# A Fourier-mixing and feed-forward kernel: a new order of work in its opening

## The chip, the cores and the metric

The kernel runs on one core of a Trainium2 chip. A core has a matrix engine (TensorE, PE in the profile, with its weight loads as PEld), three engines for element-wise work (VectorE or DVE, ScalarE or ACT, GpSimd or POOL), and SyncE (SP), which here only issues transfers. Each engine works through its own instructions in order and waits on semaphores that others raise. Transfers are issued by SP and by POOL and are carried out by 16 DMA engines. The metric is the device time of one execution in microseconds; lower is better.

## The reference

```python
# attention block: x is (8, 3008, 256), float32
X = np.fft.fft(x, axis=1)
X = np.fft.fft(X, axis=2)
attn_out = X.real.astype(np.float32)
# feed-forward block on (24064, 256); w_in is (256, 2048), w_out (2048, 256), both float64
h = x @ w_in
relu6 = np.clip(h + 3.0, 0.0, 6.0)
g = h * relu6 / 6.0
return (g @ w_out).astype(np.float32)
```

So: the real part of a two-dimensional Fourier transform over sequence and model dimension, and then a two-layer network with a hard-swish between the layers. The weights arrive as 64-bit floating point numbers, which the kernel turns into 32-bit ones itself.

## The kernel before, in words

**Pairs and stages.** The 8 sequences are worked as 4 pairs (`Pair`, `NP`). A position in a sequence of 3008 is split as 47 × 64. For each pair, `load_x` brings x in eight chunks (`NXC`), each as two transfers on POOL's queue: `load_forward` (a plain one) and `load_partners` (an indirect one, which fetches the mirrored positions by a list of rows, IX). Since only the real part is wanted, a position and its mirror image are added first: `fold` (L160) does that with five additions and subtractions a chunk (four more small ones in the last chunk, number 7). `stage1` (L214) multiplies by the 47-point transform F on PE, `evict_z` (L230) copies the result z to SBUF on ACT and writes it to DRAM (zd), `turn_column` sends one column of it apart (zq). `load_g` (L261) reads it back, with the 64 other positions now on partitions, in six groups of four frequencies; `stage2` (L271) does the 64-point transform with the table T, and `spread` (L290) puts one odd column on all partitions (qn).

**Chunks of the network.** A pair has 12 chunks of 256 columns (`Chunk`), and a chunk has 8 steps (fc). In a step, `mlp1` (L324) multiplies by W1 on PE and gives u and v in PSUM (a ring of three banks, tag uv); Vector forms s (with qn and the column table WN), u + s and v − s; ACT applies a relu to each (L376); Vector's `gate` (L379) makes the activations a of 256 frequencies and of their 256 mirror images. `mlp2` (L395) accumulates the second product over the 8 steps. It uses a scheme of seven products in place of the eight of a 2 × 2 block product: w_out is held in G as seven combinations of its blocks, and `combine` (L381, on POOL) forms four combinations c of the activations. Each product is one matmul of 256 columns. After the eighth step ACT copies the sums to e, `finish` (POOL) puts them together, `store` turns and writes them. The 384 steps of the four pairs run in one list: step s issues `mlp1` of step s + 2, `combine` of s + 1 and `mlp2` of s, and `beside` (L700) places the next pair's x, folds (on POOL), stage 1 and stage 2 between them.

**The weights.** Both weight matrices come in 16 pieces of 128 × 512 numbers (`PIECES`, 0.52 MB each): eight of w_in and eight of w_out. A piece is loaded on POOL's queue (`load_w`), and then converted by four engines in turn: `exponent_a` (ACT, two operations), `exponent_b` (PE, two 16-bit matmuls), `exponent_c` (ACT), `mantissa` (Vector, two operations), and `join` (Vector, multiplies the two). Two pieces of w_in are then multiplied with the transform over the model dimension (`fold_w_in`, four matmuls, wps), copied to W1 by ACT, and one row of the result goes to WN by way of DRAM (two transfers). Two pieces of w_out are combined by `mix_w_out` (L556, four operations on Vector).

**The opening.** For the first pair there is no earlier work to hide anything. The loop over the eight chunks issues `load_x` of chunk c + 2 and `load_w` of piece c + 2, then folds chunk c, converts piece c and does stage 1 of chunk c, so x and weights come in turns. For seven of the eight chunks `fold_first` does only three operations on Vector, and `stage1_first` does the rest of the fold on PE, with four matmuls for each half of a chunk and a negated table FN. Pieces 8 to 14 follow in a second loop, and piece 15 beside the first two steps. `keep_awake` issues matmuls whose result nobody uses. Only when the pieces are through do stage 2 of group 0 and the first `mlp1` run. In this opening the PSUM banks of the later sums (ps_a, four) serve as `bank`.

**What sets the order.** It is written out by hand: each engine runs its instructions in the order in which the code calls them. POOL's queue also holds the x and weight loads; the trace shows a load waiting there until the one eight issues before it has landed.

Of the kernel before, what the change touches and what calls it, by code (L numbers as in the profile page):

```python
# [48 lines left out]
WS = 2.0 ** 20  # L49
N1, N2 = 47, 64  # L50
NK1 = (N1 + 1) // 2

PROD = ("P1", "P2", "-P4", "P5", "P7", "-P6", "P3")
# [3 lines left out]
def kernel(  # L57
# [69 lines left out]
    def x_tile(pr, i):  # L127
        pool, tag = xpool, "x"
        if pr.p == 0 and 4 <= i < 13:
            pool, tag = ((apool, "a"), (cpool, "c"), (spool, "t"))[(i >= 8) + (i >= 11)]  # L130
        return pool.tile([PR + 2, XC, D], F32, tag=tag, name="xt")
# [8 lines left out]
    def load_forward(pr, c):  # L140
        xt = x_tile(pr, 2 * c)
# [9 lines left out]
    def load_partners(pr, c):  # L151
        xr = x_tile(pr, 2 * c + 1)
# [31 lines left out]
    def fold_first(pr, c):  # L184
        xt, xr = pr.x[c][0:PR], pr.xr[c][0:PR]
        r = xr[:, ::-1, :]
        y = ypool.tile([PR, XC + 1, D], F32, tag="y", name="y")
        tt = nc.vector.tensor_tensor
        tt(y[:, 0:XC, 1:P], xt[:, :, D - 1:P:-1], r[:, :, 1:P], op=AL.add)
        tt(xt[:, :, 1:P], xt[:, :, 1:P], r[:, :, D - 1:P:-1], op=AL.add)  # L190
        tt(xt[:, :, 0:P + 1:P], xt[:, :, 0:P + 1:P], r[:, :, 0:P + 1:P], op=AL.add)
        pr.y[c] = y

    def stage1_first(pr, c, i):
        sl = slice(2 * i, 2 * i + 2)
        a, b = pr.x[c][0:PR, sl, :], pr.y[c][:, sl, 1:P]
        ps = bank([P, 2, D], "ps1")
        for k, (f, m, c0) in enumerate([(F[0:PR, 0:PZ], a[:, :, 0:P + 1], 0), (F[0:PR, 0:PZ], b, 1),
                                        (F[0:PR, 0:PZ], a[:, :, 1:P], P + 1), (FN[0:PR], b, P + 1)]):
            nc.tensor.matmul(ps[0:PZ, :, c0:c0 + m.shape[2]], f, m, start=(k == 0), stop=(k > 0),  # L200
                             skip_group_check=True)
        evict_z(pr, c, i, ps)
        if i == XC // 2 - 1:
            del pr.x[c], pr.xr[c]


# [23 lines left out]
    def evict_z(pr, c, i, ps):  # L230
        if i == 0:

            pool, tag = (gpool, "g") if pr.p == 0 and c % 3 == 2 else (zpool, "z")
            pr.z[c] = pool.tile([PZ, XC, D], F32, tag=tag, name="z")
            if c == 0:
                pr.zd = dpool.tile([2, NK1, 2, NS, D], F32, tag="zd", name="zd")
                pr.zq = dpool.tile([2, NK1, 2, NS], F32, tag="zq", name="zq")
# [67 lines left out]
    class Chunk:  # L305
# [3 lines left out]
        def __init__(self, pr, ck):  # L309
            self.pr, self.ck = pr, ck  # L310
            self.last = ck == NCK - 1
            self.final = self.last and pr.p == NP - 1
# [81 lines left out]

    def mlp2(ch, fc):  # L395
# [78 lines left out]
    FN = wpool.tile([PR + 2, PZ], F32, tag="FN", name="FN")  # L474
# [10 lines left out]
    def load_w(j):  # L485
        kind, n, i = PIECES[j]
        st = wpool.tile([P, 2 * WB], I32, tag="st", bufs=4, name="st")
# [23 lines left out]
    def exponent_b(j):  # L511
        ex = ps_h.tile([P, WB], F32, tag="uv", name="ex")
# [17 lines left out]
    def join(j):  # L530
# [8 lines left out]
        b12 = wpool.tile([P, 2, P], F32, tag="b12", bufs=2, name="b12")[:] if i == 0 else None  # L539
        for h, g in enumerate((block(n, 0), b12) if i == 0 else (block(n, 1), block(n, 6))):  # L540
            f, e = (t.rearrange("p (c q h e) -> h p c q e", c=2, h=2, e=DH)[h] for t in (frac, ex))
            nc.vector.tensor_tensor(g.rearrange("p c (q e) -> p c q e", e=DH), f, e, op=AL.mult)
        if i == 0:
            w[PIECES[j]] = b12
# [4 lines left out]
    def use_pair(j):  # L549
        kind, n, _ = PIECES[2 * j]  # L550
        if kind == "in":
            fold_w_in(n)
        else:
            mix_w_out(n)

    def mix_w_out(j):  # L556

        b12 = w.pop(("out", j, 0))
        g = [block(j, i) for i in range(7)]
        tt = nc.vector.tensor_tensor  # L560
        tt(g[3], g[0], b12, op=AL.subtract)
        tt(g[5], g[6], g[3], op=AL.add)
        tt(g[2], g[5], g[1], op=AL.subtract)
        tt(g[4], g[6], b12, op=AL.subtract)

    def fold_w_in(n):
# [4 lines left out]
        for blk in range(2):  # L571
            ps = bank([P, WB], "wps")
# [4 lines left out]
        def copy():  # L577
            for blk in range(2):
                nc.scalar.copy(W1[:, blk, cs], sums[blk][:])
            nc.sync.dma_start(out=wn[n:n + 1], in_=W1[P - 1:P, 1, cs])  # L580

        copies.append(copy)


    def load_wn(n):
        nb = WB // P
        nc.sync.dma_start(out=WN[:, n * nb:(n + 1) * nb], in_=wn[n].rearrange("(j p) -> p j", p=P))
# [6 lines left out]
    def keep_awake(n):  # L594
        ps = ps_h.tile([P, 2 * TB], F32, tag="uv", name="awake")
# [6 lines left out]
    keep_awake(6)  # L602
# [8 lines left out]
    nc.scalar.mul(FN[:], F[:, 0:PZ], -1.0)  # L611
# [10 lines left out]
    wn = dpool.tile([NWI, WB], F32, tag="wn", bufs=1, name="wn")  # L622


    load_forward(first, 0)
    load_partners(first, 0)
    load_w(0)
    load_x(first, 1)
    load_w(1)

    pending, copies = [], []

    def on_scalar(j):
        for i in pending:
            exponent_c(i)
        if j is not None:
            exponent_a(j)
# [3 lines left out]
    def on_vector(j):  # L643
        if j is not None:
            mantissa(j)
        for i in pending:
            join(i)

    def on_tensor(j):
        if j is not None:  # L650
            exponent_b(j)
        done = pending.pop() if pending else 0
        if done % 2:
            use_pair(done // 2)
        if j is not None:
            pending.append(j)

    for c in range(NXC):
        if c + 2 < NXC:
            load_x(first, c + 2)  # L660
        load_w(c + 2)
        if c < NXC - 1:
            fold_first(first, c)
        else:
# [186 lines left out]
```

## Time and profile before

| quantity | value |
|---|---|
| median of 4 runs (lowest to highest) | 1982.1 us (1979.73 to 1984.23) |
| profiled execution, its own time | 1980.91 us |
| its span, first to last instruction | 1979.1 us |
| mean granted PE clock | 0.995 of full speed |
| one fold operation on Vector, 508 elements (L172) | 0.68 us |
| exponent operations on ACT: L509, L518 | 0.75 (two a piece), 0.58 us |
| a wps matmul of 512 columns, two instructions of 0.43 | 0.86 us |
| fetch of x, one transfer of 384 KB, issue to landing, in the steady part (median) | 4.0 us |

The profile's rows have these forms. In the list of waits: engine, line, what it waited for, then the total in us, how many times, and the longest. In the stretches: from and to, length, busy time of PE, PEld, DVE, ACT and POOL with instruction counts, the granted clock, the busy share of the DMA engines and GB/s. In the chain in order of time: start, length, and what the chain ran through. In the timeline: start, length, engine, line and operation, and in brackets the idle time before it and what ended it. A matmul on 32-bit numbers counts as two instructions; their times overlap, so 0.86 us for 512 columns is the distance from one to the next. In the transfers by queue: packets, MB, and the time the packets took as a share of 16 engines over the stretch.

### The profile page before, as it was taken

Reading aid. Unit: us, or ns where it says so; the run is one execution under the profiler, and the core shown is the slowest. Engines: PE = TensorE matmul, PEld = TensorE weight load, DVE = VectorE, ACT = ScalarE, POOL = GpSimd, SP = SyncE. Lnnn points to the kernel's source line nnn. Section 1 sums busy time; section 2 is a strip of 40 time slices with the busy share of each in tenths; the row PEclk is TensorE's granted clock in tenths of the full one; section 3 lists DMA queues with packets and bytes.
Section 4 is the critical chain, followed back from the end, with each engine's and each line's share of the span. In section 5 each row is a group of like instructions: output and inputs, shape, how many; then the busy total and the mean of one; then the engine's idle time right before and its main releaser. Section 6 shows DMA issues by size and latency. Waiting matters only on the chain.

```text
span 1979.1 us, 27746 instructions
## 1 busy us (share of the span) xinstructions
PE 1949.1 (98%) x9178; PEld 1686.8 (85%) x9178; DVE 1435.1 (73%) x2775; ACT 688.0 (35%) x1164; POOL 1412.5 (71%) x1604
## 2 busy tenths in 40 slices
PE   9899999999999999999999999999999999999998
PEld 5488888888998888888898888888889888888887
DVE  5677767776787776776777776777678777777776
ACT  6533333333333333333333333333333333333332
POOL 4277778786687787777768877778667667666765
PEclk9999999999999999999999999999999999999999
DMA  9502211121112111120111221212110101111000
GB/s 283 160 25 62 51 40 46 48 50 35 27 36 51 41 48 49 51 62 24 36 33 30 63 50 47 57 41 54 37 22 22 30 13 26 26 24 28 17 20 20
DMA packets 149701, 93.31 MB, mean 47 GB/s; under 512 B 121739, under 2 KB 135055, under 8 KB 149558
## 3 DMA queue, kind: packets, MB, share of 16 engines
q1 hardware_dynamic: 139294, 57.86, 12.3%
q0 software_dynamic: 9472, 33.49, 6.1%
q8 instruction: 72, 1.18, 0.3%
q14 instruction: 71, 0.58, 0.1%
q10 hardware_dynamic: 792, 0.20, 0.0%
HBM read 54.19 MB, written 37.33 MB: 46 GB/s over the span
## 4 chain that ended last, share of the span: by engine, by line
PE 93%; DVE 2%; ACT 1%; issue 0%; DMA 0%; SPq 0%; DVEq 0%; ACTq 0%
PE acc L403 56%; PE v L334 16%; PE u L334 16%; PE ps L284 2%; PE ps L227 2%; DVE a L379 1%; DVE s L339 1%; ACT t L376 0%; ACT PM L509 0%; DVE o L461 0%; PE wps L574 0%; DVE u L360 0%; DMA out_dram<-o 0%; PE ps L224 0%; PE awake L597 0%
## 5 line engine op out<-in xcount | busy, mean ns | idle before, releaser
L393 POOL TENSOR_TENSOR c<-a 128x512 f32<-128x512 f32 (+1 forms) x383 | 477.7, 1247 | 434.5 <-PE acc L403 371.7
L403 PE MATMUL acc<-c,G 128*128 128x256 f32 (+1 forms) x3072 | 712.1, 375 | 0.0
L376 ACT ACTIVATE t<-u,half 128x512 f32<-128x512 f32 (+1 forms) x384 | 260.7, 679 | 1101.8 <-DVE u L349 1022.0
L403 PEld LDWEIGHTS acc<-c,G 128*128 128x128 f32 x3072 | 577.9, 190 | 72.7
L339 DVE SCALAR_TENSOR_TENSOR s<-qn,WN,u 128x256 f32<-128x256 f32 (+1 forms) x768 | 330.4, 472 | 355.3 <-PE u L334 355.0
L403 PE MATMUL acc<-a,G 128*128 128x256 f32 (+1 forms) x2304 | 552.1, 375 | 0.0
L403 PEld LDWEIGHTS acc<-a,G 128*128 128x128 f32 x2304 | 434.3, 190 | 55.9
L334 PE MATMUL v<-q,W 127*128 127x256 f32 (+1 forms) x1536 | 390.0, 376 | 4.5 <-DVE a L379 4.4
L334 PE MATMUL u<-q,W 128*128 128x256 f32 (+1 forms) x1536 | 388.9, 376 | 2.4 <-DVE a L379 2.1
L379 DVE SCALAR_TENSOR_TENSOR a<-t,u 128x512 f32<-128x512 f32 (+2 forms) x448 | 264.1, 601 | 103.9 <-ACT t L376 101.8
L334 PEld LDWEIGHTS u<-q,W 128*128 128x128 f32 x1536 | 286.2, 190 | 58.2 <-issue 14.8
L334 PEld LDWEIGHTS v<-q,W 127*128 127x128 f32 x1536 | 288.6, 190 | 45.1 <-DVE a L379 4.1
L393 POOL TENSOR_TENSOR c<-c,a 128x256 f32<-128x256 f32 (+1 forms) x383 | 274.3, 716 | 30.0
L393 POOL TENSOR_TENSOR c<-a,c 128x256 f32<-128x256 f32 (+1 forms) x383 | 274.1, 716 | 30.0
L349 DVE TENSOR_TENSOR u<-s,v 128x512 f32<-128x512 f32 x352 | 245.0, 696 | 37.7 <-PE v L334 0.8
L379 DVE SCALAR_TENSOR_TENSOR a<-t,v 128x512 f32<-128x512 f32 (+1 forms) x480 | 263.8, 566 | 0.0
L376 ACT ACTIVATE t<-v,half 128x512 f32<-128x512 f32 (+1 forms) x384 | 260.3, 678 | 0.0
L351 DVE TENSOR_TENSOR v<-v,s 128x512 f32<-128x512 f32 x352 | 244.2, 694 | 0.0
L393 POOL TENSOR_TENSOR r<-w,e 128x256 f32<-128x256 f32 (+1 forms) x94 | 90.7, 986 | 3.7
L411 ACT ACTIVATE e<-acc 128x512 f32<-128x512 f32 (+2 forms) x190 | 86.2, 544 | 3.4 <-PE acc L403 3.3
L461 DVE STREAM_TRANSPOSE o<-r 128x256 f32<-128x256 f32 (+1 forms) x192 | 72.5, 416 | 0.2
L239 ACT COPY z<-ps 96x512 f32<-96x512 f32 x64 | 37.1, 580 | 82.6 <-PE ps L227 63.4
(91 smaller groups left out, 779.2 us busy)
## 6 DMA issues: line engine op xcount, KB each, us to landing
out_dram<-o SPq DMA_DIRECT2D x746, 32.0 KB
zd<-z SPq DMA_DIRECT2D x32, 384.0 KB
g<-zd SPq DMA_DIRECT2D x48, 256.0 KB
xt<-in_x_dram POOLq DMA_DIRECT2D x21, 384.0 KB, 4.0
qn<-qd SPq DMA_DIRECT2D x19, 256.0 KB
st<-in_moe_w_in_dram POOLq DMA_DIRECT2D x8, 512.0 KB, 11.1
st<-in_moe_w_out_dram POOLq DMA_DIRECT2D x8, 512.0 KB, 4.9
xt<-in_x_dram POOLq DMA_DIRECT2D x7, 376.0 KB, 4.0
```

The lines of the kernel that those rows point to most:

```text
L227: nc.tensor.matmul(ps[0:PZ], F[0:PR, 0:PZ], y[:, 2 * i:2 * i + 2, :], start=True, stop=True)
L284: nc.tensor.matmul(ps[:, blk, u * P:n].rearrange("p (b k) -> p b k", b=2), g[:, kk, blk * (P + 1):blk * (P + 1) + P], T[:, :, gr, blk, kk, ...
L334: nc.tensor.matmul(ps[:, i, 0:nq], W1[r, blk, f * P:(f + 1) * P], q[r, blk, of:of + nq], start=True, stop=True)
L339: nc.vector.scalar_tensor_tensor(s[:, i, 0:nq], qn[:, of:of + nq], WN[:, f:f + 1], u[:, i, 0:nq], op0=AL.mult, op1=AL.add)
L349: nc.vector.tensor_tensor(u[:], s[:], v[:], op=AL.add)
L351: nc.vector.tensor_tensor(v[:], v[:], s[:], op=AL.subtract)
L376: nc.scalar.activation(t, h, AF.Relu, bias=half[:], scale=scale)
L379: nc.vector.scalar_tensor_tensor(dst, t, 1.0, h, op0=AL.min, op1=AL.mult)
L393: (eng or nc.gpsimd).tensor_tensor(out, in0, in1, op=AL.add)
L403: nc.tensor.matmul(ch.acc[i // 2][:, i % 2, 0:ch.n], G[:, i, fc, :], mv, start=(fc == 0 and i % 2 == 0), stop=(fc == NF - 1), skip_group_c ...
L411: nc.scalar.mul(ch.e[:, k:i + 1, 0:ch.n], ch.acc[i // 2][:, 0:i + 1 - k, 0:ch.n], 1.0 / WS)
L461: nc.vector.transpose(o[:, 0:n // DH, h], ch.r[:, m, h, 0:n].rearrange("p (j i) -> p j i", i=DH))
```

## The change

Only the opening and the first chunk of the first pair change; the order of the steps after that is as before, with the next pair's loads placed a little differently beside the first pair.

- x comes first: six chunks of x and half of the seventh are issued before any weight, starting with chunk 7; the rest and weight pieces 0 to 3 follow after the first two folds, pieces 4 to 6 after the folds of chunks 3 and 4 (they use other buffers).
- `fold_first` and `stage1_first` go: every chunk is folded on Vector alone by `fold`, and stage 1 is the plain matmul. One `keep_awake` matmul follows each chunk.
- After x, pieces 0 to 4 are converted one after the other (with two `keep_awake` matmuls each), then come stage 2 of group 0, `spread`, and the first `mlp1`. Pieces 5 and 6 stand before the first step, three pieces (7 to 9, 10 to 12) in each of the first two steps, two in the third, one in the fourth (`DUE`).
- The first chunk uses eight plain block products (`mlp2_first`: four matmuls of 512 columns a step), which need no `combine`, no `finish`, and of G only the four plain blocks. It issues `mlp1` one step ahead. `mix_w_out` moves from Vector to POOL, into steps 4 to 6 and 9.
- WN is filled by four direct transfers for each `fold_w_in` instead of two through DRAM.

```diff
-    def fold_first(pr, c):
...
-    def stage1_first(pr, c, i):
...
+    def mlp2_first(ch, fc):
+        a = ch.a.pop(fc)
+        for h in range(2):
+            if fc == 0:
+                ch.acc[h] = ps_a.tile([P, 2, TB], F32, tag="acc", name="acc")
+            for f in range(2):
+                nc.tensor.matmul(ch.acc[h][:], G[:, (B11, B12, B21, B22)[2 * f + h], fc, :], a[:, :, f],
+                                 start=(fc == 0 and f == 0), stop=(fc == NF - 1 and f == 1))
+        if fc == NF - 1:
+            ch.r = epool.tile([P, 2, 2, TB], F32, tag="r", name="r")
+            for h in range(2):
+                for m in range(2):
+                    nc.scalar.mul(ch.r[:, m, h], ch.acc[h][:, m], (1 - 2 * m) / WS)
...
+        pool, tag, bufs = (wpool, "st", 4) if j % 7 < 4 else (cpool, "c", None)
+        st = pool.tile([P, 2 * WB], I32, tag=tag, bufs=bufs, name="st")
...
-        tt = nc.vector.tensor_tensor
-        tt(g[3], g[0], b12, op=AL.subtract)
+        tt = nc.gpsimd.tensor_tensor
+        tt(g[4], g[B22], g[B12], op=AL.subtract)
...
-            nc.sync.dma_start(out=wn[n:n + 1], in_=W1[P - 1:P, 1, cs])
+            nb = WB // P
+            for k in range(nb):
+                f = n * nb + k
+                nc.sync.dma_start(out=WN[:, f:f + 1], in_=W1[P - 1:P, 1, f * P:(f + 1) * P])
...
-    keep_awake(6)
+    keep_awake(9)
...
+    def head(j):
+        exponent_a(j)
+        mantissa(j)
+
+    def tail(j):
+        exponent_b(j)
+        exponent_c(j)
+        join(j)
+        if j + 7 < len(PIECES):
+            load_w(j + 7)
+        if j % 2 and PIECES[j][0] == "in":
+            folds.append(PIECES[j][1])
...
+    order = [NXC - 1] + list(range(NXC - 1))
+    for c in order[0:6]:
+        load_x(first, c)
+    load_forward(first, order[6])
+    for k, c in enumerate(order):
+        for part in range(2):
+            fold(first, c, part, nc.vector)
+        for i in range(XC // 2):
+            stage1(first, c, i)
+        keep_awake(1)
+        if k == 0:
+            load_partners(first, order[6])
+        elif k == 1:
+            load_x(first, order[7])
+            load_t(0)
+            for j in range(4):
+                load_w(j)
+        elif k in (4, 5):
+            for j in ((4, 5), (6,))[k - 4]:
+                load_w(j)
     load_g(first, 0)
+    head(0)
+    for j in range(5):
+        exponent_b(j)
+        keep_awake(2)
+        exponent_c(j)
+        fold_all()
+        if j < 4:
+            head(j + 1)
+        join(j)
+        copy_all()
+        load_w(j + 7)
+        if j % 2 and PIECES[j][0] == "in":
+            folds.append(PIECES[j][1])
     for i in range(2):
         stage2(first, 0, i)
     spread(first, 0)
...
+    DUE = [(7, 8, 9), (10, 11, 12), (13, 14), (15,), (), (), (), ()]
+    head(5)
     mlp1(*chunk(0))
-    mlp1(*chunk(1))
+    tail(5)
+    head(6)
+    keep_awake(3, spare[0])
+    tail(6)
...
+        if s < NF:
+            for j in DUE[s][:1]:
+                head(j)
+            copy_all()
+            mlp1(*chunk(s + 1))
+            for j in DUE[s][:1]:
+                tail(j)
+            for j in DUE[s][1:2]:
+                head(j)
+            mlp2_first(*chunk(s))
+            for j in DUE[s][1:2]:
+                tail(j)
+            for j in DUE[s][2:]:
+                head(j)
+            fold_all()
+            for j in DUE[s][2:]:
+                tail(j)
+            if 4 <= s < NF - 1:
+                mix_w_out(s - 4)
+            if s == NF - 1:
+                mlp1(*chunk(NF + 1))
+                combine(*chunk(NF))
```

## The prediction

> **What bounds the kernel now.** I read the page first: engines' busy time, then the chain of work that ended last.
>
> ```profile
> span 1979.1 us, 27746 instructions
> ...
> PE 1949.1 (98%) x9178; PEld 1686.8 (85%) x9178; DVE 1435.1 (73%) x2775; ACT 688.0 (35%) x1164; POOL 1412.5 (71%) x1604
> ...
> PE 93%; DVE 2%; ACT 1%; issue 0%; DMA 0%; SPq 0%; DVEq 0%; ACTq 0%
> ```
>
> From about 110 us on, PE (TensorE) never waits: the end is the moment at which steady steps begin, plus a fixed amount of matmul work. The change touches the opening, so I read the busy time in stretches of 10 us, whose last three columns are the granted PE clock, the DMA share and GB/s.
>
> ```profile
> 10.00:20.00 10.00, 8.79 (x25) 5.80 (x26) 5.96 (x12) 4.74 (x8) 4.94 (x8) 0.66 1.03 264
> 20.00:30.00 10.00, 10.00 (x40) 6.20 (x39) 5.75 (x12) 7.03 (x14) 3.90 (x6) 1.00 1.04 280
> 50.00:60.00 10.00, 8.03 (x27) 4.16 (x28) 7.59 (x18) 7.12 (x14) 2.14 (x3) 1.00 0.94 298
> 80.00:90.00 10.00, 5.73 (x21) 3.83 (x20) 7.62 (x14) 4.81 (x8) 4.17 (x5) 0.88 0.12 26
> 90.00:100.00 10.00, 10.00 (x37) 8.32 (x37) 5.86 (x11) 2.24 (x4) 5.45 (x6) 0.78 0.25 73
> ```
>
> The transfer engines are full until about 60 us. Then, in order of time, the chain (start, us, what):
>
> ```profile
> 61.65 1.42 ACT PM L509 x2
> ...
> 63.48 3.43 PE wps L574 x8
> ...
> 77.01 1.78 PE ps L284 x16
> 78.79 0.91 PE ps L295 x8
> ...
> 88.35 2.07 PE u L334 x4
> 90.42 1.71 PE v L334 x4
> 92.13 4.25 PE acc L403 x14
> ...
> 98.11 3.02 PE acc L403 x14
> ...
> 130.15 3.02 PE acc L403 x14
> ```
>
> Three numbers follow. The first mlp1 starts at 78.79 + 0.91 = 79.7. The eighth step's products end at 133.2, so the first chunk takes 53.5 us: eight steps of 4.74 (0.86 + 0.86 + 3.02) are 38; the rest is waits at 82 to 92 and 106 to 110, and the half clock around 88 to 94. All later work is equal in both kernels except where I name it.
>
> **The change, part by part.** A: until x has been folded. The waits name the limit, and the timeline dates it:
>
> ```profile
> DVE y L189 <- DMA xt<-in_x_dram,IX: 14.2, 7, 6.1
> ```
> ```profile
> 9.79 0.68 DVE L189 TENSOR_TENSOR y<-xt 94x508 f32<-94x508 f32 x1 [6.06 <-DMA xt<-in_x_dram,IX]
> ...
> 42.66 0.68 DVE L189 TENSOR_TENSOR y<-xt 94x508 f32<-94x508 f32 x1 [1.58 <-DMA xt<-in_x_dram,IX]
> ```
> ```profile
> q0 software_dynamic: 320, 1.16, 74.0%
> ```
>
> Folds begin at 9.8, 14.6, 19.5 and 24.5: 4.85 us for one chunk of x (0.79 MB) and one weight piece (0.52 MB). Without the piece, by bytes, a chunk is 2.9 us. But the last row (the POOL queue from 48 to 52 us, no x in it) moves 1.16 MB in 0.74 × 4 us, 392 GB/s: there a piece costs 1.34 us, which leaves 3.5 for the chunk. I take 3.3, nearer the second, because its row has weights alone. z writes (0.39 MB, 1.0 to 1.2 us each) share the engines from the third chunk on; five or six fall before the last x, and T's first group costs 1.1 more. The last chunk lands at 9.9 + 7 × 3.3 + 5.5 × 1.0 + 1 = 39.5 us (before: 48). Vector now does 5 operations a chunk, four of 0.68 overlapping to 2.65 us, 3.0 in the odd chunk with its four extra ones: under 3.3, so hidden by the transfers except after the last. POOL issues x without the pieces in between; the two x loads that need a folded chunk's buffer are queued after the first two folds (13 and 16 us), while over 3 MB are still in flight, so they cost nothing; if those transfers ran faster they would cost what the issue needs, under 2 us. The four weight loads behind them on POOL, and the next three, hold up nothing that is needed sooner. PE's work on x falls from 1.73 to 0.86 a bank (fold on Vector instead of the FN products), all of it under the transfers before and after; so do the three more awake matmuls at the start and the eight between the chunks.
>
> B: five pieces before the first step. After the last x: fold 2.65, stage 1 on PE 1.72 (two of 0.86), z copy and column on ACT 0.9, so the first exponent (L509) starts at 44.8; 1.41 and 0.4 later its matmuls are done, 46.6. From there a piece without a fold costs the chain's ACT to PE to ACT turn, 2.36 (68.73 to 71.09 in the timeline); with a fold PE holds it: two awake matmuls 1.72, wps 3.43, ex 0.45 = 5.6; the last has no next ex, 5.15. Sum 46.6 + 3 × 2.36 + 5.6 + 5.15 = 64.4, then stage 2 and spread 1.78 + 0.91: the first mlp1 starts at 67.1. Group 0's load is issued when the last z has landed, about 50 (before, 5.4 us after the z write), and 0.5 MB lands near 55: hidden by the folds of the weights. WN's direct 512-byte transfers have no row; an x load that had the engines to itself, 768 times as long, landed 4.0 us after its issue (the median of the page's list of transfers), so each lands at most that long after the copy that ends at 65. The multiply-add that needs it is due at 69: I take nothing, bounds 0 and 1. SP now issues sixteen WN transfers (0.4 to 0.6 each) instead of eight, with group 1's loads and T's behind them; these are needed at step 7, 40 us on. Gain of the opening: 79.7 − 67.1 = 12.6 us.
>
> C: the first chunk. PE per step: mlp1 1.73 and four products of 512 columns at 0.86, 3.44 instead of 3.02, so 5.2 us; no combine on POOL, which removes the 1.27 + 0.73 + 0.73 wait ahead of the c products. But eleven pieces are now converted inside it, each 2.0 on ACT (1.41 + 0.58), 1.8 on Vector (0.43 + 0.69 + 0.69), 0.45 on PE. They stand in line with the step's own: two relu 1.38 on ACT, 3.55 on Vector, and each `exponent_b` is queued on PE ahead of the products, each `exponent_c` on ACT behind the relus. Laid out along ACT: 7.0 from the first mlp1 to piece 6's `exponent_c` (qn copy 0.6, then 3.3 to the end of the first relus, 0.6 + 1.4 + 0.45 + 0.6 for the rest). In a step, a piece takes a turn of 1.41 + 0.45 + 0.58 = 2.45. The step's first `exponent_c` waits behind the relus, which wait for mantissa 1.1, s 0.85, u and v 1.3: 3.45 after its exponent instead of 0.45, so +3.0. Where a weight fold of 3.43 stands on PE ahead of the third ex, it ends 1.45 after that exponent. Steps 0 and 1: 3 × 2.45 + 3.0 + 1.45 = 11.8 each (step 1's W1 copies, 1.16 on ACT, fall into the 3.0); step 2: 2 × 2.45 + 3.0 = 7.9; step 3 is level with PE, 5.3; then PE bounds, three of 5.2 and one of 6.1 with group 1's stage 2. Sum 65.5 us. POOL's `mix_w_out` in steps 4 to 6 and 9 (four of 0.73) meets an idle POOL, and takes 1.7 per pair off Vector; the slow ones of before at 101.6 to 105 (0.83 to 1.48 each beside POOL's work, and 2.3 us of PE wait behind them) go.
>
> Still owed at that point: mlp1 of step 9, 1.73, which before had already run, and group 1's second stage-2 half, 0.89. And three mlp1 now stand almost back to back (steps 8 to 10) on three uv buffers; the third waits for the gates of the first: 1.5 (bounds 0 and 2.1, the wait at 86). So C costs 65.5 + 1.7 + 0.9 + 1.5 − 53.5 = +16.1.
>
> The clock: PE sat idle 2.15 us before 11.2, and the clock fell to 0.66 in that stretch; idle 2.1 us before 88.35 with 1.8 shortly ahead, and it fell to 0.78. Two us before 50.8 cost nothing. The new opening has PE idle about 1.8 us in every 4.4 while x arrives (stage 1 1.72 + awake 0.86 busy). If the last of these chunks runs at half clock it costs 1.7; if the first weight fold does too, 1.7 more. Bounds 0 and 3.4; I take 0.9, a quarter.
>
> The Trainium skill speaks here, "TensorE: Matmul & The Clock Gate", Part 1: PE falls to half clock after at least one idle window of about 3.4 us. By that rule no gap of the new opening is long enough, and the sum would be 0.9 lower; the rows above show the fall after gaps of 2.1 us, so the rows decide.
>
> Sum: −12.6 + 16.1 + 0.9 = +4.4 us on the profiled execution's 1980.9 (span 1979.1 and 1.8 around it), that is 1985.3. Its time is 1.2 under the median 1982.1, so against the median: 1986.5. A measurement can hardly tell 0.2%, 4 us.
>
> **The rivals.** 1, on the other side: x alone runs faster than between weights. If a chunk took the 2.0 us of the 392 GB/s row, the last would land at 9.9 + 7 × 2.0 + 6.5 = 30.4, and its fold would end at 33 instead of 42 (Vector alone, 7 × 2.65 after the first, allows 31.5). The weights follow in time: pieces 0 to 4 at 1.34 us each and two z writes are there by 40. 9 us earlier is 1977.5. It decides from 2.6 us a chunk on (7 × 0.7 = 4.9 us against the 4.4). For it: 392 GB/s is reached; against: four intervals in a row fit 3.3 to 3.5.
> 2, the clock falls in the first chunk too: steps 0 to 2 leave PE gaps of 1.0 to 1.5. The fall at 88 held into the next stretch, and cost u, v and acc (2.07 + 1.71 + 4.25 against 0.86 + 0.86 + 3.02) 3.3 us. Once here and in full while x arrives: 1986.5 − 0.9 + 3.3 + 3.4 = 1992. For it: the gaps are many; against: three awake matmuls are placed there, and a gap of 1.8 alone at 82.8 cost nothing.
> 3, the order doesn't change in effect: z writes delay x so that it lands at 46, as before. Then the opening gains 6 us, 1993. Against it: the writes are 3 MB of 9.5.
>
> **How the numbers follow.** Forecast 0.50, rival 1 0.28, rival 2 0.18, rival 3 0.04. The forecast's own spread is the x price (2.9 to 3.5: −2.8 to +1.4), the clock (−0.9 to +2.5), the uv wait (−1.5 to +0.6) and 2 us for the layout: 1981 to 1991, half of it beyond 1986.1 (the median and 0.2%). So slower 0.27 + 0.22 = 0.49; within 0.2% 0.23 + 0.16 = 0.39; faster, from rival 1 at its full price, 0.12. The range takes in most of rivals 1 and 2: 1978 to 1993.
>
> **What would show it.** Folds (now L170) starting 3.3 apart, then 4.3, the last near 39.5; first L509 at 45; first u matmul at 67; PE gaps of about 1 us before ex in steps 0 and 1, each step 11.8; u of step 10 waiting for a gate. The prediction is wrong if the last fold starts before 35 or after 43, if steps 0 and 1 take under 10 or over 13 us, or if the clock falls between 65 and 105.

## The result and the profile after

The changed kernel takes 1985.27 us (median of 39 runs, 1983.75 to 1988.12), the kernel before 1981.01 us beside it: a ratio of 1.002, 95% interval 1.0016 to 1.0025. It is 4.3 us slower, 0.2%; the prediction had called that hard to tell, and over this many runs it is clear. The forecast was 1986.5, and its sum for the difference was +4.4 us. The profiled execution took 1985.56 us, with a span of 1983.8.

So the difference came out to 0.1 us. The parts did not: several missed, and by luck they cancel. The page of the changed kernel first (busy time, then shares of the chain that ended last):

```profile
span 1983.8 us, 27522 instructions
...
PE 1951.8 (98%) x9076; PEld 1665.7 (84%) x9076; DVE 1437.3 (72%) x2773; ACT 687.4 (35%) x1163; POOL 1398.2 (70%) x1591
...
PE 93%; DVE 3%; DMA 2%; ACT 1%; issue 1%; POOL 0%; SPq 0%; DVEq 0%; ACTq 0%
```

PE is busy 2.7 us longer and the span is 4.7 us longer; DMA has gone from 0 to 2% of the chain. Two lines of the chain in order of time make up more than half of that, 22.45 us (start, us, what):

```profile
18.42 10.45 DMA zd<-z
...
30.04 12.00 DMA zd<-z
```

Those are writes of z. The prediction had expected the landing of x to set the opening, and the folds of x in Vector's timeline show that x is early:

```profile
9.89 0.55 DVE L170 TENSOR_TENSOR xt<-xt 94x381 f32<-94x381 f32 x1 [6.07 <-DMA xt<-in_x_dram,IX]
...
22.56 0.68 DVE L170 TENSOR_TENSOR xt<-xt 94x508 f32<-94x508 f32 x1 [0.39 <-DMA xt<-in_x_dram,IX]
...
33.79 0.68 DVE L170 TENSOR_TENSOR xt<-xt 94x508 f32<-94x508 f32 x1 [1.36 <-DMA xt<-in_x_dram,IX]
```

The last fold starts at 33.8, not 39.5. ACT's timeline shows who waits instead:

```profile
28.95 1.06 ACT L220 COPY z<-ps 96x512 f32<-96x512 f32 x2 [3.75 <-DMA zd<-z]
...
39.28 1.06 ACT L220 COPY z<-ps 96x512 f32<-96x512 f32 x2 [7.32 <-DMA zd<-z]
...
42.12 1.07 ACT L220 COPY z<-ps 96x512 f32<-96x512 f32 x2 [1.44 <-DMA zd<-z]
...
43.43 1.37 ACT L508 ACTIVATE PM<-st,bias 128x512 uint8<-128x512 int16 x2
```

A z copy needs a free z buffer. A buffer is free when its write to DRAM has landed, and these landed 10 to 12 us after their issue. ACT waits 12.5 us in three places, and the first exponent, which stands behind the last z copy on ACT, starts at 43.4. PE meanwhile has nothing to do. Its rows, and the granted clock in the stretches of 10 us (the third number from the end):

```profile
44.21 1.22 PE L513 MATMUL ex<-PM,E 128*128 128x512 f16 x2 [4.73 <-ACT PM L508]
...
67.26 1.03 PE L316 MATMUL u<-q,W 128*128 128x256 f32 x4
...
75.91 3.59 PE L385 MATMUL acc<-a,G 128*128 128x512 f32 x8
...
80.45 0.85 PE L513 MATMUL ex<-PM,E 128*128 128x512 f16 x2 [0.95 <-DVE wi L534]
...
87.39 3.59 PE L385 MATMUL acc<-a,G 128*128 128x512 f32 x8
...
98.85 3.59 PE L385 MATMUL acc<-a,G 128*128 128x512 f32 x8
...
106.52 3.59 PE L385 MATMUL acc<-a,G 128*128 128x512 f32 x8
...
135.80 1.13 PE L316 MATMUL v<-q,W 127*128 127x256 f32 x4 [1.54 <-DVE a L361]
```
```profile
10.00:20.00 10.00, 9.25 (x28) 3.93 (x28) 8.79 (x20) 2.93 (x6) 6.43 (x8) 1.00 1.03 246
20.00:30.00 10.00, 8.47 (x20) 2.86 (x19) 7.68 (x16) 3.98 (x8) 4.34 (x7) 1.00 1.04 313
30.00:40.00 10.00, 7.45 (x17) 2.54 (x16) 7.05 (x14) 2.38 (x7) 1.15 (x2) 1.00 1.03 363
40.00:50.00 10.00, 5.74 (x11) 2.32 (x11) 1.96 (x4) 5.97 (x12) 1.08 (x2) 0.66 0.98 356
...
70.00:80.00 10.00, 8.88 (x26) 4.09 (x24) 9.09 (x18) 7.35 (x12) 1.79 (x3) 1.00 0.54 150
```

The first mlp1 starts at 67.26 (forecast 67.1). Products of steps 0 to 3 start at 75.9, 87.4, 98.9 and 106.5: intervals of 11.48, 11.46 and 7.67 (forecast 11.8, 11.8, 7.9). The clock falls to 0.66 between 40 and 50, behind the idle 4.73 us, and is 1.00 from 50 on.

The last part of the difference lies later, where the prediction had not looked. In both kernels a few matmuls of the next pair's stage 1 wait for ACT. Before, then after, PE's timeline:

```profile
270.03 1.10 PE L227 MATMUL ps<-y,F 94*96 94x512 f32 x2 [0.67 <-ACT q L287]
...
453.25 1.10 PE L227 MATMUL ps<-y,F 94*96 94x512 f32 x2 [0.57 <-ACT q L287]
...
553.31 0.90 PE L334 MATMUL v<-q,W 127*128 127x194 f32 x4 [0.48 <-DVE a L379]
```
```profile
190.81 1.10 PE L208 MATMUL ps<-y,F 94*96 94x512 f32 x2 [0.68 <-ACT q L268]
...
273.00 1.10 PE L208 MATMUL ps<-y,F 94*96 94x512 f32 x2 [0.68 <-ACT q L268]
...
355.20 1.10 PE L208 MATMUL ps<-y,F 94*96 94x512 f32 x2 [0.68 <-ACT q L268]
...
437.39 1.10 PE L208 MATMUL ps<-y,F 94*96 94x512 f32 x2 [0.68 <-ACT q L268]
...
557.73 0.89 PE L316 MATMUL v<-q,W 127*128 127x194 f32 x4 [0.20 <-DVE a L361]
```

Beside the first pair there are four such places instead of two. The last row of each fence is the same matmul of the first pair's last chunk, and so a common mark: 557.73 − 553.31 = +4.4 us. Later batches add 0.2.

### The profile page after: what moved, and what is told of

The parts are those of the page before. It is cut to its first block, busy times and chain, and to the rows that moved or that the text cites. A ratio compares the mean times of both kernels' runs of the same rounds, so it can differ in the third digit from the quotient of the medians.

```text
span 1983.8 us, 27522 instructions
## 1 busy us (share of the span) xinstructions
PE 1951.8 (98%) x9076; PEld 1665.7 (84%) x9076; DVE 1437.3 (72%) x2773; ACT 687.4 (35%) x1163; POOL 1398.2 (70%) x1591
## 4 chain that ended last, share of the span: by engine, by line
PE 93%; DVE 3%; DMA 2%; ACT 1%; issue 1%; POOL 0%; SPq 0%; DVEq 0%; ACTq 0%
PE acc L401 55%; PE v L316 16%; PE u L316 16%; PE ps L265 2%; PE ps L208 2%; DMA zd<-z 1%; PE acc L385 1%; DVE a L361 1%; DVE s L321 1%; ACT t L358 0%; ACT PM L508 0%; DMA xt<-in_x_dram,IX 0%; DVE o L459 0%; PE wps L563 0%; PE spare L563 0%
## 5 line engine op out<-in xcount | busy, mean ns | idle before, releaser
L375 POOL TENSOR_TENSOR c<-a 128x512 f32<-128x512 f32 (+1 forms) x375 | 467.4, 1246 | 409.1 <-PE acc L401 360.6
L401 PE MATMUL acc<-c,G 128*128 128x256 f32 (+1 forms) x3008 | 696.9, 374 | 0.0
L401 PEld LDWEIGHTS acc<-c,G 128*128 128x128 f32 x3008 | 565.4, 190 | 71.1
L401 PE MATMUL acc<-a,G 128*128 128x256 f32 (+1 forms) x2256 | 539.1, 375 | 0.0
L401 PEld LDWEIGHTS acc<-a,G 128*128 128x128 f32 x2256 | 424.2, 190 | 54.4
L375 POOL TENSOR_TENSOR c<-c,a 128x256 f32<-128x256 f32 (+1 forms) x375 | 268.4, 716 | 29.4
L375 POOL TENSOR_TENSOR c<-a,c 128x256 f32<-128x256 f32 (+1 forms) x375 | 268.2, 715 | 29.4
L208 PE MATMUL ps<-y,F 94*96 94x512 f32 x120 | 61.3, 601 | 9.5 <-ACT q L268 5.2
```

What stands on the lines that cost most here:

```text
L208: nc.tensor.matmul(ps[0:PZ], F[0:PR, 0:PZ], y[:, 2 * i:2 * i + 2, :], start=True, stop=True)
L375: (eng or nc.gpsimd).tensor_tensor(out, in0, in1, op=AL.add)
L401: nc.tensor.matmul(ch.acc[i // 2][:, i % 2, 0:ch.n], G[:, i, fc, :], mv, start=(fc == 0 and i % 2 == 0), stop=(fc == NF - 1), skip_group_c ...
```

## The experiments

The theory from the two traces: z's buffers hold the opening, by some 4 us; the half clock behind them costs 1 to 2 us; the eleven conversions inside the first chunk cost more than anything else; and stage 1 stands too close behind stage 2. Rivals are named with each run. Each time carries the ratio to the kernel before with its 95% interval. The kernel before was measured again beside each group of runs, and its median lay between 1981.0 and 1982.7 us; so a difference of under 2 us between two runs is read only where the traces show it.

**1. More z buffers.** Three chunks of the opening put their z into buffers of another pool that is still unused.

```diff
+            if pr.p == 0 and c in (3, 5, 6):
+                pool, tag = qpool, "q"
             pr.z[c] = pool.tile([PZ, XC, D], F32, tag=tag, name="z")
```

> The changed kernel with three of the first pair's eight z tiles in the q buffers, which nothing uses before stage 2, so that no z copy waits for an earlier z to have landed in DRAM. Theory 1, the opening ends late because ACT's z copies wait for the z writes (12.5 us in three waits, the last x is folded at 36.4 but the first exponent starts at 43.4): the waits go, the first exponent starts at 37.5 to 38.5, PE's idle time after the last stage 1 falls from 4.7 us to under 2, the clock stays at 1.00, first u matmul at 59 to 61 instead of 67.4, total 1977 to 1979, 6 to 8 us under the changed kernel and 2 to 4 under the one before. Theory 2, as in the prediction, the arrival of x and the weights sets the opening: the copies start earlier but the exponents wait for weight pieces instead, the first u matmul stays within 2 us of 67.4, total 1983 to 1986.

Measured 1981.02 us (1.0000, 0.9991 to 1.0009), 4.2 us under the changed kernel. The waits for z's writes are gone, and ACT's timeline shows the next one, on the four buffers of the copied column, whose small writes stand in the same queue:

```profile
35.91 0.30 ACT L237 ACTIVATE zc<-z,F 96x4 f32<-96x4 f32 x1 [2.59 <-DMA zq<-zc]
...
38.88 0.30 ACT L237 ACTIVATE zc<-z,F 96x4 f32<-96x4 f32 x1 [1.72 <-DMA zq<-zc]
39.09 1.38 ACT L510 ACTIVATE PM<-st,bias 128x512 uint8<-128x512 int16 x2
```

The first exponent comes 4.3 us sooner, the first mlp1 at 62.80 instead of 67.26. The cause is settled: the opening waited for z buffers. The gain fell short of the expected time (1977 to 1979), because of this second wait and because x's own end is close by: the last fold starts at 31.7, from which copies without any wait would lead to a first exponent at 37.0. The expectation also had PE's idle time under 2 us and the clock at 1.00. The idle time is 2.49 us, and the four awake instructions behind it take 3.43 us instead of 1.88:

```profile
39.88 0.38 PE L515 MATMUL ex<-PM,E 128*128 128x512 f16 x1 [2.49 <-ACT PM L510]
...
40.74 3.43 PE L587 MATMUL awake<-Z,ones 128*128 128x512 f32 x4
```

**2. The clock.** Five awake matmuls in PE's idle time ahead of the first exponent, nothing else.

```diff
     load_g(first, 0)
+    keep_awake(5)
```

> The changed kernel with five more idle matmuls of 0.86 us after the last stage 1, which bridge PE's 4.7 us gap. If the half clock of 44 to 49 us (an ex of 1.22 and two awake matmuls of 3.53 in place of 0.8 and 1.88) lies on the path, the first u matmul comes 1.5 to 2.0 us earlier, at 65.5, and the total falls by as much, to about 1983.5. If the ACT chain hides it, no change.

Measured 1984.42 us (1.0014, 1.0005 to 1.0023), 0.9 less than the changed kernel; the two intervals overlap, so the trace has to show it. The clock is 1.00 from 40 to 50, with the z waits as long as before (13.4 us). ACT's first exponent and PE's first mlp1:

```profile
43.89 1.38 ACT L508 ACTIVATE PM<-st,bias 128x512 uint8<-128x512 int16 x2
```
```profile
66.14 1.03 PE L316 MATMUL u<-q,W 128*128 128x256 f32 x4
```

The first mlp1 starts 1.1 us sooner although the first exponent started 0.5 later: the way between them takes 22.25 us instead of 23.83. The half clock is real and worth 1.6 us there.

**3. No conversions in the first chunk.** Pieces 7 to 15 are neither loaded nor converted (G, W1 and WN are filled with zeros first), so part of the weights is left out of the result; pieces 5 and 6 stay.

```diff
     def head(j):
+        if j >= 7:
+            return
...
     def tail(j):
+        if j >= 7:
+            return
...
```

> The changed kernel without pieces 7 to 15: they are neither loaded nor converted, and the blocks of W1, WN and G that would hold them are zero from memory sets on POOL in the opening. It measures what the eleven conversions cost the first chunk. Theory of the prediction (three conversions in a step make a chain over ACT, PE and Vector of 11.8 us instead of PE's 5.2): the first chunk, from the first u matmul to the end of the eighth step's products, falls from 64.3 us to about 50, steps 0 to 3 take 5.2 each, total 14 us lower, near 1971. Rival (the first chunk is bound by its eight products and by mlp1 one step ahead): under 4 us lower.

Measured 1969.2 us (0.9937, 0.9922 to 0.9952). The first mlp1 starts at 66.88, nearly where it was, the steps take 5.17 us each, and the products of step 7 start at 112.03 instead of 128.07. With 0.38 taken off for the earlier start, nine conversions and the two weight folds that go with them cost the first chunk 15.7 us, 1.7 a piece. That is the price that the change pays for an opening that is 12.3 us shorter.

**4. Two pieces a step.** The nine pieces spread 2, 2, 2, 2, 1 instead of 3, 3, 2, 1.

```diff
-    DUE = [(7, 8, 9), (10, 11, 12), (13, 14), (15,), (), (), (), ()]
+    DUE = [(7, 8), (9, 10), (11, 12), (13, 14), (15,), (), (), ()]
```

> The changed kernel with the eleven pieces of the first chunk spread as 2, 2, 2, 2, 1 over its first steps (after the two around the first mlp1) instead of 3, 3, 2, 1. Theory: the third piece of a step costs 11.47 - 7.67 = 3.8 us because the step's second and third exponents wait in line behind its own relus and the weight fold; two pieces cost 7.7. Then steps 0 to 3 take 7.7 each and step 4 about 5.3: 36 us instead of the 41 that the changed kernel's steps 0 to 4 take, so 1980 to 1981, 4 to 5 us faster. Rival: ACT's and Vector's work for eleven pieces is the limit wherever they stand; then the first chunk keeps its 64 us and the time stays at 1985.

Measured 1988.77 us (1.0033, 1.0020 to 1.0046): slower, a miss. PE's timeline has the products of steps 0 to 4 start at

```profile
75.79 3.60 PE L385 MATMUL acc<-a,G 128*128 128x512 f32 x8
...
86.63 3.60 PE L385 MATMUL acc<-a,G 128*128 128x512 f32 x8
...
99.33 2.84 PE L385 MATMUL acc<-a,G 128*128 128x512 f32 x6 [2.04 <-DVE G L540]
...
104.81 3.59 PE L385 MATMUL acc<-a,G 128*128 128x512 f32 x8
...
112.82 3.60 PE L385 MATMUL acc<-a,G 128*128 128x512 f32 x8
```

(step 2 at 96.26, with the 2.04 us of wait inside it). From step 0 to step 4 that is 37.0 us, against 35.8 in the changed kernel (75.91 to 111.68). A piece of w_out that moves to the head of its step makes the products wait for its join. The theory "a third piece costs 3.8 us because it is the third" falls: spread this way, the same work costs no less. The profiled execution took 1986.47 us, less than the other five, and its trace explains 1.1 us; the rest of the median's 3.5 stays open.

**5. The gap before the first chunk of the kernel before.** Two awake matmuls in each of two places around its first mlp1s, to see whether its idle 2.1 us cost it the half clock.

```diff
     mlp1(*chunk(0))
+    fill(2)
     mlp1(*chunk(1))
     on_tensor(15)
+    fill(2)
```

> The kernel before with two idle matmuls between its first two mlp1 and two after piece 15's exponent matmuls, where PE waits at 82.8 to 84.7 and 86.2 to 88.4. If the half clock at 88 to 94 comes from these gaps and lies on the path, u, v and the first products of that stretch take 0.9, 0.9 and 3.0 us instead of 2.07, 1.71 and 4.25, and the total falls by about 3 us, to 1978. If the clock falls for another reason, no change or up to 1 us more.

Measured 1978.99 us (0.9982, 0.9972 to 0.9993). In the stretches and in PE's timeline of this run:

```profile
80.00:90.00 10.00, 9.34 (x48) 6.79 (x47) 6.23 (x13) 5.26 (x9) 1.77 (x2) 1.00 0.20 62
90.00:100.00 10.00, 9.59 (x43) 7.81 (x42) 7.67 (x14) 3.48 (x6) 7.89 (x10) 1.00 0.26 79
```
```profile
91.14 1.13 PE L334 MATMUL u<-q,W 128*128 128x256 f32 x4 [0.41 <-DVE a L379]
92.11 1.03 PE L334 MATMUL v<-q,W 127*128 127x256 f32 x4
```

The clock stays at 1.00; u and v take 0.97 and 0.87 instead of 2.07 and 1.71, and acc 3.02 instead of 4.25. 3 us of the kernel before were half clock behind its two gaps of 1.84 and 2.12 us. Both were filled here, so the run does not say which of them did it.

**6. Weights issued later.** In program order, all seven pieces of the opening behind the seventh fold.

```diff
-            for j in range(4):
-                load_w(j)
-        elif k in (4, 5):
-            for j in ((4, 5), (6,))[k - 4]:
+        elif k == 6:
+            for j in range(7):
                 load_w(j)
```

> All seven weight pieces of the opening are issued after the seventh chunk's fold instead of after the second to the sixth, so x and the z writes have the transfer engines to themselves. Theory: z writes land 10 to 12 us after their issue because the weights behind x keep the engines full; without them they land 4 to 6 us after it, and ACT's waits for a z buffer (12.5 us together in the changed kernel) fall under 4 us, the last chunk's copies start near 37 instead of 39.3. The first weights then land at about 33 to 36, after the last fold, and the first exponent starts between 37 and 40 instead of 43.4, the kernel 2 to 5 us faster than the changed one (1981 to 1983). Rival: a z write takes its 10 us whatever else is in flight; then the waits stay at 12 us and the kernel stays at 1985 or, with the weights late, becomes slower.

Measured 1985.89 us (1.0015, 1.0006 to 1.0025), ACT's waits unchanged at 12.5 us. It decides nothing, since the edit moved almost nothing: the first piece is issued at 22.42 instead of 21.51, because POOL runs through its list ahead of the folds and is held by earlier landings only.

**7. Weights really held back.** The same, with a small POOL copy that reads the sixth folded chunk ahead of them.

```diff
+        if k == 5:
+            seen = wpool.tile([P, 1], F32, tag="seen", bufs=1, name="seen")
+            nc.gpsimd.tensor_copy(seen[0:PR], first.y[c][:, 0, 0:1])
```

> The changed kernel with the opening's seven weight pieces held back by a small copy on GpSimd that reads the sixth folded chunk: the pieces are then issued from about 29 on, where the changed kernel issues six of them from 21.5 to 30 whatever its program order, since an issue waits for the landing of an earlier transfer. Theory: the z writes are late (10 to 12 us after their issue) because they share the engines with eight loads in flight; with x alone in flight from 21 to 29 and its queue running empty, the third to sixth land 5 to 7 us after their issue, ACT's three waits for a z buffer (12.5 us together) fall below 6, the first exponent starts at 39 to 41 instead of 43.4 unless the first weights, due near 35, are late: 1981 to 1983. Rival: the writes are slow by themselves; the waits stay at 12 us and the time at 1985 or above.

Measured 1981.56 us (0.9996, 0.9987 to 1.0005), 3.7 less than the changed kernel, and the first exponent at 39.80, both as expected. But the waits fall only to 8.4 us, and the chain of waits still shows slow writes:

```profile
19.39 9.99 DMA zd<-z
...
30.55 7.86 DMA zd<-z
```

The first was issued and landed before any weight piece was in flight; POOL's timeline has the first pieces at

```profile
29.62 2.16 POOL L489 DMA_DIRECT2D st<-in_moe_w_in_dram  x4
```

The second, with weights behind x now in flight, took 7.86 us where it had taken 12.00. So weights that come sooner make later writes slower, but beside x alone a write needs 10 us too.

**8. Column buffers as well.** Run 1 with eight column buffers instead of four, and three awake matmuls ahead of the first exponent.

```diff
-        zc = zpool.tile([PZ, XC], F32, tag="zc", bufs=4, name="zc")
+        zc = zpool.tile([PZ, XC], F32, tag="zc", bufs=8, name="zc")
...
+    keep_awake(3)
```

> On top of the run with three more z buffers: eight buffers instead of four for the copied columns, and three awake matmuls ahead of the first exponent. Theory: with z no longer the limit, the columns' four buffers were (waits of 2.6 and 1.7 us on ACT before the last chunks); without them the first exponent starts at about 37 instead of 39.1 and the first mlp1 near 60.5 instead of 62.8, and the three matmuls save another 0.5 to 1 us of half clock: 1978 to 1979. Rival: the next wait behind it is the landing of the last z write and so of group 0; then stage 2 waits and the first mlp1 stays at 62 to 63, the time at 1981.

Measured 1981.15 us (0.9995, 0.9986 to 1.0005): no gain over run 1, a miss. No buffer wait is left, but in this run the last x landed later and the awake matmuls held up the first ex. Rows of Vector and ACT:

```profile
34.09 0.68 DVE L170 TENSOR_TENSOR xt<-xt 94x508 f32<-94x508 f32 x1 [1.67 <-DMA xt<-in_x_dram,IX]
```
```profile
39.77 1.39 ACT L510 ACTIVATE PM<-st,bias 128x512 uint8<-128x512 int16 x2
...
42.82 0.58 ACT L519 ACTIVATE ex<-ex 128x512 int32<-128x512 f32 x1 [1.66 <-PE ex L515]
```

The last fold starts at 34.1, against 31.7 in run 1. Of these 2.4 us, 1.1 are there at the first fold (10.06 against 8.97), before any z was written; that the z writes, which now go out sooner, take the rest from x is likely but was not shown. Now the landing of x is the limit that the prediction had supposed. The rival named for this run, the landing of group 0, was not it.

**9. Stage 1 one step later.** Beside the changed kernel's later steps only.

```diff
-                    put(t + 8 + 3 * i, stage1, nx, c, i)
+                    put(t + 9 + 3 * i, stage1, nx, c, i)
```

> The changed kernel with the next batch's stage 1 one step later in the later chunks, so that it no longer stands in the same step right behind a stage 2 of the present batch. Theory: of the 4.3 us that the changed kernel is slower, 1.4 are two more waits of 0.68 us of PE for the copy of stage 2's bank (at 190.8 and 355.2, beside the one at 273 that the kernel before has at 270); all three go, 2.0 us faster: 1983. Rival: the waits were slack of PE that is given back later (a buffer that comes free in time); then the time stays at 1985.

Measured 1980.7 us (0.9988, 0.9979 to 0.9998), 4.6 less than the changed kernel; 2.0 had been expected. Of the eight places in all, six are gone: PE's timeline has none of the four waits of the first pair left, one instead of two in each of the next two, and the common mark:

```profile
554.47 0.90 PE L316 MATMUL v<-q,W 127*128 127x194 f32 x4 [0.20 <-DVE a L361]
...
766.82 1.10 PE L208 MATMUL ps<-y,F 94*96 94x512 f32 x2 [0.68 <-ACT q L268]
...
1240.30 1.10 PE L208 MATMUL ps<-y,F 94*96 94x512 f32 x2 [0.68 <-ACT q L268]
```

The mark comes 3.26 sooner although this run's first mlp1 came 0.38 later: 3.64 for four places, 0.91 each, so a place costs more than its wait of 0.68. The two later pairs are 0.76 shorter each. The size was off because three places had been counted.

**10. The same in the kernel before.**

```diff
-                    put(9 * c + 8 + 3 * i, stage1, nx, c, i)
+                    put(9 * c + 9 + 3 * i, stage1, nx, c, i)
```

> The kernel before, with nothing but the next batch's stage 1 one step later. Theory: a stage 1 right behind a stage 2 costs about 0.9 us of PE (0.68 of wait and some 0.2 around it), and the kernel before has two such places in each of three batches, the shifted one fewer: 2 to 3 us faster, 1979 to 1980. With that the changed kernel's two more places in the first batch are worth 1.9 us of its 4.3. Rival: the gain of the same shift in the changed kernel came from something else in its first batch; then the kernel before stays at 1982.

Measured 1980.62 us (0.9988, 0.9979 to 0.9997), 1.3 less by the medians and 2.4 by the ratio. In its trace one place is left in each pair; the later two pairs take 473.47 and 473.48 us instead of 474.24 and 474.23, 0.76 less each, as in run 9. The first pair of the profiled execution starts late: its products of step 1 come at 100.42 instead of 98.11, 2.3 us later, behind a clock of 0.66 in the stretch from 50 to 60. Its last chunk's mark comes only 1.55 later (554.86 instead of 553.31), so this pair too gains 0.76. That confirms the mechanism at 0.76 a pair, 2.3 us in all, inside the interval of the times.

**11 and 12. Together.** Run 1's buffers, eight column buffers, stage 1 apart, and the second half of group 1's stage 2 in front of the v matmuls that wait 1.54 us; then the same with the weights held back as in run 7.

```diff
-                put(t + 3 + 4 * i, stage2, pr, gr, i)
+                put(t + 3 + (1 if pr is first and gr == 1 else 4) * i, stage2, pr, gr, i)
```

> The changed kernel with what the runs so far point to, together: three more z buffers and eight column buffers in the opening (no added awake matmuls), the next batch's stage 1 one step later, and the second half of group 1's stage 2 three steps sooner, ahead of the v matmuls that wait 1.5 us for a gate. Theory: the terms add, since they stand in different stretches: -4.2 (buffers), -4.6 (stage 1 apart), -0.9 (stage 2 inside the wait of 1.54, of which 0.6 is left): 1975 to 1977, 5 to 7 us under the kernel before. Rival: what is saved in the opening is taken back by x itself, which landed between 31.7 and 34.1 in the two runs with more buffers; then the first mlp1 stays at 64 to 66 and the time is 1978 to 1980.

> The best version so far (buffers, stage 1 apart, stage 2 in the wait) with the seven weight pieces held back as in the run before. Theory: with the buffer waits gone the opening is set by the landing of x, whose last chunk's fold started at 34.7 with the weights in flight behind it and at 32.9 with the weights held back; so the first exponent starts near 39.3 instead of 41.1, the first mlp1 near 61.6 instead of 63.4, and the time falls by 1.5 to 2 to 1972 to 1973. Rival: the weights, issued at 29 and later, land too late for the first folds of the weights, and the opening ends where it did, or later: 1974 to 1977.

Measured 1974.39 us (0.9958, 0.9944 to 0.9971) and 1973.54 us (0.9957, 0.9943 to 0.9970). The terms add: 9.7 us less than the changed kernel was the expected sum, 10.9 was measured. The wait for the gate shrinks from 1.54 to 0.64, as computed. In the second, the first exponent starts at 39.66 and the first mlp1 at 61.92 (expected 39.3 and 61.6; 63.37 without the hold); the 0.85 us between the two medians is inside their intervals, so only the trace speaks for the hold. Both beat the kernel before by about 8 us and the changed one by 11 to 12. What cost the new order its gain were buffers and neighbours that it had not been fitted to. The 8 us are not all the order's own, though: the kernel before gains 3.2 us by run 5 and 1.3 to 2.4 by run 10. No run has both together; if they add, it would come to some 1977 us (an estimate), 3 to 4 above the last run.

## Why the prediction came out right

The forecast of +4.4 and the mark's +4.4 have different parts, and that they agree is luck: 2.0 us that the prediction did not name are set off by an opening and a first chunk that were 1.8 us better than forecast. At the mark, from PE's timelines of the two traces:

| part | forecast | measured |
|---|---|---|
| opening, up to the first mlp1 (half clock in it) | −12.6 + 0.9 | 67.26 − 79.52 = −12.26 |
| first chunk | 65.5 − 53.5 = +12.0 | 64.24 − 53.49 = +10.75 |
| mlp1 of step 9 | +1.7 | +1.7 |
| wait for a gate at step 10 | +1.5 | +1.5, and 0.3 around it |
| second half of stage 2 | +0.9 | +0.9 |
| stage 1 right behind stage 2 in the first pair | not named | 4 × 0.91 − (0.91 + 0.76) = +2.0, at the prices of runs 9 and 10 |
| wait at the mark | not named | 0.20 − 0.48 = −0.3 |

The first chunk counts up to the matmul behind the eighth step's products. The right column sums to 4.6; the mark shows 4.4.

**Part A failed in its cause.** "The last chunk lands at 39.5" came from two prices. A chunk at 3.3 us was right (intervals 3.1 to 3.6, the last 4.1). Adding 5.5 z writes at 1 us each, and T's load at 1, was wrong: all of them pushed x back by 0.8 us (33.8 against 9.9 + 7 × 3.3 = 33.0), not 6.5. The working took the transfer engines as full; at the same busy share of 1.03 to 1.04 they moved 246 GB/s from 10 to 20 and 313 from 20 to 30, so most of z came on top. The last fold started at 33.8, below the 35 that the prediction named as a sign that it is wrong. The step "z copy and column on ACT 0.9" had no term for the buffers. By the prediction's own chain (2.65 + 1.72 + 0.9 behind the last fold) the first exponent would have started at 39.1; it started at 43.4, and run 1 gives back the 4.3 us (that it lands on 39.1 is chance: its x came 2.1 us earlier, and its column buffers took that back). The working had counted the DMA cost of z but not asked when a z buffer comes free. "First exponent at 44.8" was thus near, for another reason.

**Part B** took 23.8 us from the first exponent to the first mlp1, forecast 22.3. The 1.5 more is the half clock: in run 2, without it, the same way takes 22.25. The prediction had priced it at 0.9 but placed it on the last chunks of x or the first weight fold; it fell on the first pieces, behind a gap (4.73 us) that the prediction did not foresee. The steps costed at nothing held: no wait for WN shows ahead of s, and none for group 0 ahead of stage 2. "Cost nothing" for the loads of the reused x buffers held within the last interval's 0.6 us.

**Part C** held in its layout: steps of 11.48, 11.46, 7.67, then 5.17, against 11.8, 11.8, 7.9, 5.3 and 5.2, and 1.54 for the wait. Run 3 shows the conversions past the seventh piece at 15.7 us. The one other spreading that was tried, run 4, was no cheaper. POOL's `mix_w_out` delayed nothing that PE shows: it has no wait in steps 4 to 7.

**The step that was missing** is the new place of the next pair's stage 1. The text ahead of the prediction says that the loads are placed a little differently; the prediction gave that no term and named no cover for it. It had read that PE never waits from about 110 us on; but already the kernel before has six such waits of 0.57 and 0.67 us, two beside each of the first three pairs. In the first pair four in place of two cost 2.0 us, almost half of the result.

**The rivals.** 1 (x alone is faster) got half of its way: the last fold came at 33.8, between the 30.4 of the rival and the forecast's 39.5; but not by faster transfers of x (3.1 to 4.1 us a chunk, above the 2.6 that decide), and the z buffers took it away. 2 (the clock falls in the first chunk) is out: 1.00 from 50 on, with gaps of 1.0. 3 (z delays x) is out in its size: x's last fold came at 33.8, not near 46. It was z that came late.

On the clock, the Trainium skill ("TensorE: Matmul & The Clock Gate", Part 1) names an idle window of about 3.4 us ahead of the fall. The 4.73 us of the changed kernel and its fall to 0.66 agree with that. The 2.12 us of the kernel before do not, and run 5 shows that the fall there was due to the idle time of 1.84 and 2.12 us: with both filled, the clock stays at 1.00 and 3 us are saved. Nor does run 11 agree, where the clock fell to 0.50 behind an idle time of 1.73 us. Here the runs decide.

## What to carry to other kernels

When an order is changed so that transfers are packed more tightly, ask of every buffer in the stretch when it comes free, and not only what its transfer costs: a write that lands 10 us after its issue stops a ring of four buffers, whatever its transfer costs by bytes. Compare the list of waits per tile, not only the end of the stretch, since a forecast can be right by two errors. And price each shift of a step against its new neighbours in the same step, for the whole run that repeats it: four collisions of 0.9 us in place of two made almost half of the difference.

## What the runs showed of the hardware that was not expected

- A z write of 384 KB on SP's queue landed 10.0 us after its issue before any weight was in flight (run 7), and 7.9 to 12.0 us in the other places shown. It need not take that long: the changed kernel's last one was issued at 43.21, when x had long landed and POOL's queue had weight pieces, and `load_g`, which waits for its landing, was issued 5.1 us later, at 48.29.
- The changed kernel's transfers by queue show what the early writes wait for. The first z write is issued at 15.40, but until 20.5 only POOL's queue moves packets. Then the two queues take turns. From 24 to 25 us POOL's moves 71 packets with 0.25 MB and SP's 72 packets with less than 0.01 MB; by the order of that queue these are the column writes, which stand between one z write and the next. The Trainium skill ("DMA: Bandwidth & Descriptors", Queues, rings and completion order) says that each engine takes turns between the queues it has work for, packet by packet. The 71 and 72 packets agree with that. So a z write waits while the small packets ahead of it go one for one with large packets of x. Why the first packet comes 5 us after its issue stays open.
- x arrives more slowly than the weights: 246 GB/s over the stretch from 10 to 20 us, with x alone moving, against a mean of 413 GB/s from 34 to 46 us, with weights and z in flight. Why was not tried.
- Idle times of PE of 1.73, 1.94, 2.12, 2.15, 2.49, 2.65 and 3.02 us were each followed by half clock (run 11 at 37.6, run 7 at 40.6, kernel before at 88 and at 11.2, run 1 at 39.9, run 5 at 51.7, run 10 at 52.2); one of 2.02 (before, at 50.8) was not. Run 11's row, with 2.66 us for what takes 1.93 at full clock:

```profile
37.62 2.66 PE L208 MATMUL ps<-y,F 94*96 94x512 f32 x4 [1.73 <-DVE y L178]
```

  So the length of one gap does not decide alone, and the same place in the program falls on either side from one execution to the next.
